# A written-out order of one long kernel: small products of TensorE gathered, first loads reordered

## The chip, the core and the metric

The kernel runs on one core of a Trainium2 chip. Its work is done by TensorE (PE; its weight loads are PEld), VectorE (DVE), ScalarE (ACT) and GpSimd (POOL); SyncE (SP) issues the DMAs. The metric is the device time of one execution in microseconds, the median of three runs. Times inside an execution are counted from the start of its span, the time from its first to its last instruction.

## What is computed

Three layers in a row, for batch B = 2, sequence S = 768, H = 8 heads of D = 64 (model width 512):

```python
# attention: each query sees 31 neighbours and 24 block summaries
k_sum = k.reshape(B, H, 24, 32, D).max(axis=3)
v_sum = v.reshape(B, H, 24, 32, D).mean(axis=3)
scores_l = where(|i - j| < 16, scale * q @ k.T, -1e9)
scores_s = scale * q @ k_sum.T + log(32)
a = softmax(concat(scores_l, scores_s))
x = a @ concat(v, v_sum)            # (B, S, 512)
# first feed-forward block, a convolution over the sequence as gate
h = relu(x @ w_in)                  # 512 -> 1024
gate = sigmoid(conv3(h, conv_w))
x = (h * gate) @ w_out              # 1024 -> 512
# second feed-forward block, with a layer norm
xn = (x - mean) / sqrt(var + 1e-6) * g_ln
out = x + relu(xn @ w_ch1) @ w_ch2  # 512 -> 2048 -> 512
```

Weights arrive as 64-bit floats and are turned into 32-bit ones on the chip.

## The kernel before

**How it is written.** A class `Plan` holds 2016 operations. Each has a name, the engines that may do it, a function that issues its few instructions, and the operations that it comes after. Buffers that are shared in turn are rings, such as `tr` (five PSUM banks), `x2` (two) and `ch` (two). The string `ORDER` at the head of the file lists every operation once, by its number, with the engine that does it: `13S` is operation 13 on SP, `44P` is 44 on TensorE, and V, A, G are DVE, ACT, POOL. `arrange` reads the string, and `trace` issues the operations in that order under manual scheduling. So each engine gets its instructions in exactly the order in which they stand in the string, and each executes its own in that order; waits come from data and buffers.

**Attention** goes by pairs j = 0 to 11, each 128 queries; two units u = 2j, 2j+1 of four heads belong to a pair. The names in the text:

- `kt`, `qt` (L373, early ones): transposes of k and q, made as products with an identity with 64 columns of the array. `kmb` (L394): maxima of k over blocks, on DVE. All six `kmb` of the first batch come ahead of the first scores.
- `M` (L479): writes the mask into a score bank; `S` (L487): scores of a pair, 64x64 products, accumulated on the mask; `X` (L541): row maximum; `E` (L553): exponent; `N` (L572): division by the sum; `P` (L582): transposes the probabilities, full size.
- `T` (L503): product with v for a pair, with 64 columns of the array. `H` and `L` (L269, L527) split its result in two 32-bit parts for the first feed-forward block.
- M0, M1, M10 to M13, M22 and M23 stand at the ends of the sequence and are two products of 64 columns each; the other M are one full-size product.

**The first feed-forward block** has 48 steps i. `h` (L719): x times w_in, in three parts a, b, c of four matmuls each; then on ACT and DVE relu, the three taps of the convolution (`b`, `c`), tanh, the gate `g` and its two parts `u`, `v`; and `x` (L796): six full-size products with w_out into two banks, for two halves. `h` and `x` of different steps stand between attention's products, from 45 us on.

**The second block.** `bn`, `ba`, `va`, `rs`, `nb` (L1034 to L1048) make mean and scale of a row; the power -0.5 is on POOL (L1046). `xn` (L1167 on ACT, L1170 on DVE) normalises, `tp` (L1205) transposes it on TensorE. Seven products `pr` (L1264) a step stand in for eight by a Strassen scheme; their results are added up on DVE (`pb` to `ph`, L1275). `ac` (L1343) multiplies by w_ch2 into accumulators. There are 16 steps, eight for each half of the batch, in an alternating order. `wa`, `wb` names are the weights' conversion (L639, L643, L648), `wo`, `wn`, `wl`, `wm` the low parts of the weights (L1075).

**The loads.** SP issues all loads in the order of the string: `lq`, `lk`, `lv` for q, k, v, `lw0` to `lw7` for w_in and `lw8` to `lw15` for w_out, each of 512 KB, `lc0` and `lc1` for the convolution's weights and the norm's.

The lines that make the string count:

```python
for word in order.split():
    o = self.ops[int(word[:-1])]
    o.eng = word[-1]
    assert o.eng in [e[0] for e in o.engs] and all(a in seen for a in o.after), o.name
    seen.add(o)
    self.done.append(o)
```

Of the kernel before, what the change touches and what calls it, by code (L numbers as in the profile page):

```python
# [8 lines left out]
104V 222V 40V 216V 199A 105A 233P 191P 204P 217V 106V 192A 51A 234P 235P 182V 101A 1P 102G 236V 243V 176A 205A 111A
159V 223V 86V 115S 237A 87A 55P 218P 177P 224V 110V 209V 88V 107A 225P 244A 108G 179V 200P 226V 238V 245V 246V 112V  # L10
228G 206P 219A 121S 201A 113A 180V 239V 247G 227P 207A 240V 114G 403P 402P 229A 202V 404P 89A 117A 230V 248P 241P 56V
412V 127S 231G 253P 413A 254P 405V 255P 424G 90G 266P 256A 232S 396S 359S 401S 242V 249V 267P 123A 406A 268P 116V 414V
122V 118V 257V 415V 279P 258V 128V 416G 280P 269A 281P 292P 282A 259V 293P 427P 417P 124V 407V 260A 426P 270A 428P
261V 283A 271V 284V 272V 294P 436V 262A 119A 120G 125A 273A 418A 305P 306P 437A 307P 126G 133S 263V 318P 139S 367S
408V 429V 274V 319P 308A 409V 295A 320P 264P 309V 430A 331P 397P 399P 296V 297V 285V 310V 438V 286A 275A 398A 431V
439V 135A 663S 425S 287V 276V 432V 311V 321A 312A 440V 265P 332P 410P 277P 333P 441P 344P 345P 134V 433V 298V 136V
322A 323V 313V 411A 129A 400A 299A 334A 288A 130V 300V 335V 324V 250P 278P 141A 131A 137A 346P 251V 140V 420G 252V
442V 289G 434P 419P 132G 290P 347A 421A 142V 138G 145S 291P 363P 368P 348A 325A 435A 301A 422V 360P 666P 423G 376S
151S 443P 667A 364A 336V 361V 302V 337V 349V 326V 350V 362V 365V 143A 444A 314A 446P 447P 369A 338A 351A 147A 315G
144G 370V 303P 448P 449A 450A 304P 352V 146V 339V 316P 459P 460P 371P 664P 372A 461P 462A 451V 445V 148V 152V 153A  # L20
327A 463G 377P 472P 328G 714S 380P 473P 149A 378A 474P 485P 317P 373V 452V 464V 383S 475A 381A 665V 465V 668G 150G
466A 340A 486P 672P 487P 329P 715P 498P 379V 382V 658V 499P 500P 453A 476A 659A 341V 154V 454V 385S 155A 501A 467V
477V 478V 502G 384V 671P 330P 156G 511P 342P 343P 488A 353A 479A 489A 694P 512P 695P 513P 386V 394V 375G 480V 387S
719S 354G 355P 357P 366G 389S 356A 503V 504V 490V 514A 673P 455A 524P 681V 505A 468A 515A 525P 456G 526P 696P 506V
374V 358V 388V 491V 457P 527A 682A 697V 528G 469G 458P 537P 481A 492A 470P 538P 698A 493V 660G 482G 539P 471P 516V
683V 684V 517V 529V 699V 674V 483P 494A 540A 395A 484P 552P 495G 496P 497P 553P 390V 530V 685G 507A 675A 518A 508G
519V 554P 555A 531A 541A 509P 510P 686P 676V 556A 520A 677V 391G 716A 565P 566P 567P 722P 721P 661V 704V 532V 705A
568A 723P 700V 678V 557V 521V 701G 689G 392V 542V 543V 393S 692S 731V 1129V 533A 544A 687A 569A 702P 679P 545V 578P
558V 724V 559A 534V 579P 580P 522P 523P 581A 732A 725A 535P 582G 560V 570V 583V 584V 706V 680V 707V 708G 591P 536P
592P 744P 720S 669S 693S 733V 670S 571V 546A 547V 726V 593P 745P 746P 703A 594A 572A 573V 747V 709P 710A 604P 605P  # L30
606P 548P 734V 735V 595A 596V 754V 736P 748A 727V 607A 585A 586V 749V 608V 550P 551V 609V 750V 617P 755A 618P 717P
619P 688P 711P 549A 620A 621A 561A 630P 562G 597V 718V 737A 598A 574A 756V 728V 729P 599V 610V 631P 871P 632P 690A
730A 633A 622V 623V 575V 691V 757V 611A 612V 751V 738P 563P 712V 713V 758V 662A 564P 872P 643P 873P 644P 587A 893G
# [1404 lines left out]
```

## Time and profile before

| | |
|---|---|
| runs (three) | 484.31, 484.78, 485.12 us; median 484.78 |
| the profiled execution | 484.99 us, its span 483.0 us |
| granted clock of TensorE, mean | 0.989 |
| busy: TensorE, DVE, ACT, POOL | 465.5, 364.6, 256.8, 124.4 us |

Busy time is the time in which an instruction of the engine runs. Matmuls follow each other in a pipeline, so one's length (391 ns for a 128x512 one) is longer than the distance to the next; what a matmul costs is read from the distance between starts. A matmul of 32-bit numbers can stand in the trace as two or more.

### The profile page before, as it was taken

To read this page: it belongs to the slowest core of one execution; us is meant where nothing else is said; L and a number is where in the kernel's file an instruction comes from. 1 tells how busy PE (TensorE), PEld (TensorE's weight loads), DVE (VectorE), ACT (ScalarE), POOL (GpSimd) and SP (SyncE) were. 2 spreads that over 40 slices of the span, in tenths; PEclk is the share of its full clock that TensorE was granted. 3 is DMA by queue.
4 is the path that set the end of the run, shared out by engine and by line. 5 is a ranking of instruction groups with operands and counts; after the bars stand their busy time and mean duration, and the time that the engine had idled before them with its cause. 6 is when DMAs were issued, how large, how long until landed. Compare 5 with 4: busy or idle time off the path is not lost.

```text
span 483.0 us, 8906 instructions
## 1 busy us (share of the span) xinstructions
PE 465.5 (96%) x3297; PEld 409.4 (85%) x3297; DVE 364.6 (75%) x776; ACT 256.8 (53%) x733; POOL 124.4 (26%) x154
## 2 busy tenths in 40 slices
PE   3999999999999999996999999999999999999997
PEld 3848888888889889885889998999899998889985
DVE  2799999998886778898798766778565768664553
ACT  4699987688676695767862425324332324322110
POOL 4545333631220331302531421102520202011000
PEclk9899999999999999997999999999999999999999
DMA  8996966404400211002201213202031120220213
GB/s 254 318 281 186 246 157 167 108 4 89 97 3 1 88 45 45 0 2 87 88 23 67 88 44 131 87 1 88 17 131 58 56 88 0 90 87 1 87 45 130
DMA packets 56043, 43.28 MB, mean 90 GB/s; under 512 B 34324, under 2 KB 46896, under 8 KB 56000
## 3 DMA queue, kind: packets, MB, share of 16 engines
q1 hardware_dynamic: 55856, 42.58, 30.8%
q8 instruction: 26, 0.43, 0.4%
q14 instruction: 17, 0.14, 0.1%
q10 hardware_dynamic: 144, 0.13, 0.1%
HBM read 39.22 MB, written 3.15 MB: 88 GB/s over the span
## 4 chain that ended last, share of the span: by engine, by line
PE 91%; DVE 3%; ACT 3%; DMA 2%; issue 1%; SPq 0%; POOL 0%; POOLq 0%; ACTq 0%
PE acc L1343 27%; PE ch L1264 23%; PE x L796 14%; PE h L719 13%; PE tr L503 2%; PE tr L582 2%; PE tr L719 2%; PE tr L487 2%; DMA early<-in_k_dram 2%; PE tr L366 1%; PE acc L1205 1%; PE tr L479 1%; PE x L841 1%; ACT xn L1167 1%; PE tr L373 1%
## 5 line engine op out<-in xcount | busy, mean ns | idle before, releaser
L1343 PE MATMUL acc<-w,cb 128*128 128x512 f32 x570 | 140.1, 391 | 0.0
L1343 PEld LDWEIGHTS acc<-w,cb 128*128 128x128 f32 x570 | 106.2, 188 | 18.8
L1264 PE MATMUL ch<-xb,w 128*128 128x384 f32 x384 | 78.1, 341 | 2.8 <-ACT xb L1239 1.4
L1264 PEld LDWEIGHTS ch<-xb,w 128*128 128x128 f32 x384 | 68.9, 190 | 6.4 <-ACT xb L1239 1.6
L719 PE MATMUL h<-xT,wi 128*128 128x256 f32 (+1 forms) x504 | 72.3, 287 | 0.0
L719 PEld LDWEIGHTS h<-xT,wi 128*128 128x128 f32 x504 | 66.7, 189 | 4.3 <-issue 0.7
L796 PE MATMUL x<-wo,ghi 128*128 128x512 f32 x192 | 61.7, 402 | 0.0
L1264 PE MATMUL ch<-xt,w 128*128 128x384 f32 x288 | 58.7, 341 | 0.0
L1275 DVE TENSOR_TENSOR u<-ch,u 128x384 f32<-128x384 f32 x64 | 35.2, 554 | 24.7 <-PE ch L1264 24.5
L1264 PEld LDWEIGHTS ch<-xt,w 128*128 128x128 f32 x288 | 51.9, 191 | 1.8
L752 DVE SCALAR_TENSOR_TENSOR c<-h,ccol,c 128x256 f32<-128x256 f32 x96 | 46.9, 500 | 3.7 <-POOL c L271 1.7
L1284 ACT ACTIVATE cb<-p 128x384 fp32r<-128x384 f32 x32 | 16.4, 519 | 45.8 <-DVE p L1275 34.4
L643 ACT ACTIVATE raw<-raw 128x512 f32<-128x512 f32 x32 | 21.4, 677 | 36.1 <-DMA raw<-in_moe_w_ch_dram 36.1
L796 PE MATMUL x<-wo,glo 128*128 128x512 f32 x96 | 38.0, 395 | 0.0
L796 PEld LDWEIGHTS x<-wo,ghi 128*128 128x128 f32 x192 | 32.2, 188 | 4.7 <-issue 0.4
L1284 ACT ACTIVATE cb<-u 128x384 fp32r<-128x384 f32 x32 | 16.3, 520 | 33.3 <-DVE u L1275 33.3
L553 ACT ACTIVATE prob<-tr,nm 128x120 f32<-128x120 f32 x96 | 33.2, 366 | 0.9 <-DVE nm L541 0.8
L731 ACT ACTIVATE h<-h 128x256 f32<-128x256 f32 (+1 forms) x42 | 16.2, 386 | 23.8 <-PE h L719 21.5
L1075 POOL TENSOR_TENSOR w<-raw,w 128x512 fp32r<-128x512 f32 (+1 forms) x12 | 15.0, 1254 | 51.2 <-ACT w L1142 45.0
L765 DVE SCALAR_TENSOR_TENSOR g<-c,h 128x256 f32<-128x256 f32 x48 | 22.5, 473 | 5.2 <-ACT c L757 5.0
L648 DVE SCALAR_TENSOR_TENSOR raw<-raw 128x512 uint32<-128x512 uint32 x32 | 23.1, 723 | 3.1 <-ACT raw L643 3.0
L783 POOL TENSOR_TENSOR glo<-g,ghi 128x256 fp32r<-128x256 f32 x19 | 15.5, 815 | 29.3 <-ACT ghi L776 21.4
(178 smaller groups left out, 772.2 us busy)
## 6 DMA issues: line engine op xcount, KB each, us to landing
raw<-in_moe_w_ch_dram SPq DMA_DIRECT2D x32, 512.0 KB, 3.4
wst<-in_moe_w_out_dram SPq DMA_DIRECT2D x8, 512.0 KB, 4.4
vw<-in_v_dram SPq DMA_DIRECT2D x20, 192.0 KB, 4.5
wst<-in_moe_w_in_dram SPq DMA_DIRECT2D x5, 512.0 KB, 7.7
s_q<-in_q_dram SPq DMA_DIRECT2D x8, 256.0 KB
early<-in_k_dram SPq DMA_DIRECT2D x3, 512.0 KB, 9.3
x2a<-in_moe_w_in_dram SPq DMA_DIRECT2D x3, 512.0 KB
early<-in_v_dram SPq DMA_DIRECT2D x3, 512.0 KB, 7.6
```

The costliest lines, as they stand in the source:

```text
L553: A.activation(out=pr[:, p, :], in_=sc[:, p * NK:(p + 1) * NK], func=AF.Exp, bias=nm[:, p:p + 1], scale=1.0, accum_out=sm[:, p:p + 1])
L643: A.activation(out=f, in_=f, func=AF.Prelu, scale=F64_SCALE, alpha=F64_SIGN)
L648: V.scalar_tensor_tensor(out=most, in0=most, scalar=3, in1=least, op0=ALU.logical_shift_left, op1=ALU.bitwise_or)
L719: T.matmul(live["h", i][:, 0:NM_], w_[:, c, f * 128:(f + 1) * 128], x_[:, c, 1:1 + NM_], start=(k_ == 0 and c == 0), stop=(k_ == 2 and c = ...
L731: A.activation(out=ht[:, lead:lead + NH], in_=live.pop(("h", i))[:, 0:NH], func=AF.Relu)
L752: V.scalar_tensor_tensor(out=ct, in0=ht[:, kk:kk + CH], scalar=ccol[:, kk * NF + f:kk * NF + f + 1], in1=ct, op0=ALU.mult, op1=ALU.add)
L765: V.scalar_tensor_tensor(out=gt, in0=ct, scalar=1.0, in1=ht, op0=ALU.add, op1=ALU.mult)
L796: T.matmul(x2ps[g, t], l[:, ts_], r[:, f, :], start=(f == 0 and j == 0), stop=(f == NF - 1 and j == 2))
L1264: T.matmul(bk[k], l[:, c, :], x_[:, c, :], start=j == 0 and c == 0, stop=j == 2 and c == 1)
L1275: lambda e: V.tensor_tensor(out=temp(to), in0=bk[k], in1=temp(x), op=ALU.add), after,
L1284: A.activation(out=half(0, r, y), in_=temp(src), func=AF.Relu)
L1343: T.matmul(acc[key], ct_[n][l][:, r, 128 * t:128 * t + 128], w2[s][k][:, r], start=first and j == 0, stop=done and j == 5)
```

## The change

Only the string `ORDER` differs: the same 2016 operations in another order, and some of them on another engine. The counts by letter go from 765 V, 476 A, 128 G, 85 S and 562 P to 751 V, 467 A, 150 G, 86 S and 562 P. Nothing else in the file is touched. Both lists keep every operation behind those that it comes after.

```diff
-13S 4G 5G 2G 8S 67S 61S 11S 10S 12S 14S 73S 91S 44P 79S 15S 7V 6V 68V 52V 69A 53A 70V 45A 46P 71A 63A 62V 64V 65A 47A
+13S 178G 2G 3G 157G 5G 67S 11S 10S 61S 12S 8S 14S 73S 44P 46P 79S 91S 15S 85S 45A 69A 68V 70V 25P 28P 71A 29A 47V 4G
...
```

SP's first loads were q0, conv, w1, w0, k1, k0, k2, q1, w2; they are now q0, w1, k1, k0, w0, k2, conv, q1, w2 (`w1` for `lw1`, and so on).

**DVE at the beginning**, from the first operation on a weight to the row maximum X0 (`nm`). `wst` is a staged piece of w_in, `ksum` the six maxima of k, `craw` the conv weights, `qb` and `kw` the scores' operands. Before:

```order
L639 TENSOR_SCALAR wst<-wst 128x512
L648 SCALAR_TENSOR_TENSOR wst<-wst 128x512
L648 SCALAR_TENSOR_TENSOR craw<-craw 24x128
L862 COPY crow<-craw 24x128
L394 TENSOR_REDUCE ksum<-tr 128x2x8
L394 TENSOR_REDUCE ksum<-x_182 128x2x8
L394 TENSOR_REDUCE ksum<-tr 128x2x8
L394 TENSOR_REDUCE ksum<-x_215 128x2x8
L394 TENSOR_REDUCE ksum<-x_224 128x2x8
L394 TENSOR_REDUCE ksum<-tr 128x2x8
L639 TENSOR_SCALAR wst<-wst 128x512
L648 SCALAR_TENSOR_TENSOR wst<-wst 128x512
```

After:

```order
L639 TENSOR_SCALAR wst<-wst 128x512
L394 TENSOR_REDUCE ksum<-x_181 128x2x8
L648 SCALAR_TENSOR_TENSOR wst<-wst 128x512
L394 TENSOR_REDUCE ksum<-tr 128x2x8 x2
L287 MEMSET warm 128x64
L394 TENSOR_REDUCE ksum<-x_209 128x2x8
L639 TENSOR_SCALAR craw<-craw 24x128
L394 TENSOR_REDUCE ksum<-x_227 128x2x8
L394 TENSOR_REDUCE ksum<-tr 128x2x8
L269 COPY kw_92<-kw_93 128x4x16
L269 COPY kw_93<-kw_92 128x4x16
L271 TENSOR_SCALAR qb_96<-tr 128x512
```

In both pieces the first row is the second weight piece, w0. Its second step now stands between the first maximum and the others, and the conv weights' last steps have gone further down.

**TensorE at the end of attention**, the two products T10 and T11 (L503; 16 products in the program's count, 32 in the trace's). Before:

```order
L719 MATMUL h<-xT,wi_87 128x258 x8
L503 MATMUL tr<-probT,vw_98 64x64 x16
L719 MATMUL h<-xT,wi_88 128x258 x4
L796 MATMUL x_2016<-wo_617,ghi 128x512
L796 MATMUL x_2016<-wo_618,ghi 128x512
L796 MATMUL x_2016<-wo_617,glo 128x512
L503 MATMUL tr<-probT,vw_99 64x64 x16
L796 MATMUL x_2515<-wo_617,ghi 128x512
```

After:

```order
L719 MATMUL h<-xT,wi_87 128x258 x8
L719 MATMUL h<-xT,wi_88 128x258 x4
L503 MATMUL tr<-probT,vw_98 64x64 x16
L503 MATMUL tr<-probT,vw_99 64x64 x16
L796 MATMUL x_2536<-wo_670,ghi 128x512
```

The two blocks of 64-column products have become one, with one border ahead and one behind.

**DVE in the change from the first to the second feed-forward block**, from the statistics of the last two row tiles (`st`, `mv`) to the normalised rows `xn` of the second half of the batch; `w` is the low part of a weight, `ts`, `sg` and `xb` belong to the first half's operands. Before:

```order
L1034 BN_STATS st<-x2b 128x6 x2
L1037 BN_AGGR mv<-st 128x2
L1075 TENSOR_TENSOR w_3300<-raw,w_3299 128x512
L1037 BN_AGGR mv<-st 128x2
L1043 TENSOR_SCALAR rs<-mv 128x6
L1075 TENSOR_TENSOR w_3300<-raw,w_3299 128x512
L1224 TENSOR_TENSOR ts<-sg,acc 128x256
L1075 TENSOR_TENSOR xb_2540<-acc,xb_2539 128x4x128
L1224 TENSOR_TENSOR ts<-sg,ts 128x256
L1048 SCALAR_TENSOR_TENSOR rs<-mv,rs 128x6
L1224 TENSOR_TENSOR ts<-acc,ts 128x256
L1170 TENSOR_SCALAR xn<-x2b,mv,rs 128x512
```

After:

```order
L1034 BN_STATS st<-x2b 128x6 x2
L1037 BN_AGGR mv<-st 128x2 x2
L1043 TENSOR_SCALAR rs<-mv 128x6
L1075 TENSOR_TENSOR w_3300<-raw,w_3299 128x512
L1224 TENSOR_TENSOR ts<-sg,acc 128x256
L1075 TENSOR_TENSOR xb_2529<-acc,xb_2528 128x4x128
L1224 TENSOR_TENSOR ts<-sg,ts 128x256
L1048 SCALAR_TENSOR_TENSOR rs<-mv,rs 128x6
L1075 TENSOR_TENSOR w_3300<-raw,w_3299 128x512
L1224 TENSOR_TENSOR ts<-acc,ts 128x256
L1170 TENSOR_SCALAR xn<-x2b,mv,rs 128x512
```

The low part of the weight (`w_3300`) that stood between the two aggregates now stands behind the variance's last step (L1043). The `xn` in the last row is the first half of its pair before, and the second half after; the other half is ACT's. On TensorE, the two groups of transposes of this pair (`tp101`, `tp100`) have a product pr001 and pr002 between them before, and follow each other after; `tp111` has moved from behind pr004 to behind pr010.

## Rows read from the trace of the kernel before

**Rows 1.** The page, part 1: busy us, share of the span, instructions.

```profile
PE 465.5 (96%) x3297; PEld 409.4 (85%) x3297; DVE 364.6 (75%) x776; ACT 256.8 (53%) x733; POOL 124.4 (26%) x154
```

**Rows 2.** Stretches: length, busy us (instructions) of PE, PEld, DVE, ACT, POOL, PEclk, DMA.

```profile
0.00:45.00 45.00, 35.44 (x488) 25.66 (x489) 32.11 (x75) 32.90 (x103) 22.81 (x46) 0.96 0.92 261
45.00:218.10 173.10, 173.10 (x1525) 152.42 (x1525) 152.38 (x351) 129.92 (x451) 50.29 (x65) 1.00 0.32 78
218.10:222.90 4.80, 2.39 (x15) 1.74 (x13) 4.59 (x13) 2.79 (x6) 2.87 (x2) 1.00 0.31 95
222.90:229.80 6.90, 5.54 (x21) 5.12 (x20) 5.16 (x11) 5.48 (x10) 0.00 (x0) 0.51 0.27 86
229.80:239.30 9.50, 8.92 (x54) 8.25 (x53) 7.82 (x17) 7.73 (x15) 5.10 (x6) 1.00 0.36 111
239.30:473.80 234.50, 234.50 (x1179) 211.87 (x1178) 159.58 (x309) 77.97 (x150) 43.30 (x38) 1.00 0.19 62
```

**Rows 3.** Waits of TensorE: us in total, times, longest us.

```profile
PE tr L373 <- DMA early<-in_q_dram: 5.1, 1, 5.1
...
PE ch L1264 <- ACT xb L1239: 1.4, 1, 1.4
PE acc L1205 <- ACT xn L1167: 1.4, 1, 1.4
PE ch L1264 <- DVE xb L1075: 1.0, 1, 1.0
```

**Rows 4.** Timeline of TensorE, 119.5 to 161.6 us: start, us, instructions.

```profile
120.72 2.08 PE L503 MATMUL tr<-probT,vw 120*64 120x64 f32 x64
122.74 0.74 PE L719 MATMUL h<-xT,wi 128*128 128x256 f32 x4
...
158.60 0.40 PE L796 MATMUL x<-wo,glo 128*128 128x512 f32 x1
158.93 1.15 PE L503 MATMUL tr<-probT,vw 120*64 120x64 f32 x32
160.01 0.74 PE L796 MATMUL x<-wo,ghi 128*128 128x512 f32 x2
160.59 0.39 PE L796 MATMUL x<-wo,glo 128*128 128x512 f32 x1
160.82 0.63 PE L796 MATMUL x<-wo,ghi 128*128 128x512 f32 x2
161.28 0.40 PE L796 MATMUL x<-wo,glo 128*128 128x512 f32 x1
```

**Rows 5.** Timeline, 0 to 30 us, with idle time before and its releaser.

```profile
6.37 0.43 DVE L639 TENSOR_SCALAR wst<-wst 128x512 uint32<-128x512 uint32 x1 [5.28 <-DMA wst<-in_moe_w_in_dram]
...
9.29 0.85 DVE L639 TENSOR_SCALAR wst<-wst 128x512 uint32<-128x512 uint32 x1 [1.50 <-DMA wst<-in_moe_w_in_dram]
...
11.09 1.77 PE L373 MATMUL x<-ident,early 128*64 128x128 f32 x16 [2.64 <-DMA early<-in_k_dram]
...
17.24 1.29 DVE L394 TENSOR_REDUCE ksum<-x 128x16 f32<-128x512 f32 x2 [0.29 <-ACT kw L267]
...
21.47 0.64 DVE L541 TENSOR_REDUCE nm<-tr 128x4 f32<-128x480 f32 x1
```

**Rows 6.** Timeline of DVE, 42 to 45 us.

```profile
43.22 1.28 DVE L527 TENSOR_TENSOR xT<-tr,xT 128x512 fp32r<-128x512 f32 x2
```

**Rows 7.** Timeline of the change of blocks, 219 to 225 us.

```profile
219.66 0.66 DVE L1075 TENSOR_TENSOR w<-raw,w 128x512 fp32r<-128x512 f32 x1
...
222.86 0.54 DVE L1170 TENSOR_SCALAR xn<-x2b,mv,rs 128x512 f32<-128x512 f32 x1
...
223.72 0.81 ACT L1167 ACTIVATE xn<-x2b,rs 128x512 f32<-128x512 f32 x1
```

**Rows 8.** The page, part 5: busy us, mean ns of one, idle before.

```profile
L1275 DVE TENSOR_TENSOR u<-ch,u 128x384 f32<-128x384 f32 x64 | 35.2, 554 | 24.7 <-PE ch L1264 24.5
...
L648 DVE SCALAR_TENSOR_TENSOR raw<-raw 128x512 uint32<-128x512 uint32 x32 | 23.1, 723 | 3.1 <-ACT raw L643 3.0
```

More of the change, by code (lines that the diff above doesn't have):

```diff
@@ L9 @@
[L9 to L33, printed above, removed]
@@ new lines @@
+1202V 1078V 1055V 1142V 1088P 1146V 1020A 1032P 1148V 1044V 1089A 1033P 1090G 1066V 1056A 1067A 1079V 1068V 1057V
+1091V 1099P 1045P 1046P 1100P 1080A 1092V 1101P 1058P 1102A 1069A 1070G 1103A 1093A 1059P 1112P 1209V 1147V 1081V
+1113P 1104V 1082A 1083V 1094V 1143V 1200V 1114P 1205A 1071P 1115A 1105V 1206G 1072P 1116A 1117V 1084P 1095A 1106A
+1149V 1096V 1085P 1107V 1118V 1097P 1108A 1119A 1201V 1109V 1098P 1120V 1207A 1121A 1110P 1210V 1122V 1111P 1208V
+1123P 1278V 1125P 1124A 1150V 1126A 1211P 1212P 1279A 1152V 1213A 1151V 1153V 1154V 1218A 1280V 1155G 1273A 1214V
@@ new lines @@
+1286S 1219V 1215V 1315P 1217G 1156V 1274V 1224A 1216V 1281S 1220A 1225V 1222A 1221G 1227P 1226P 1223V 1288A 1287V
+1317P 1289V 1228A 1316A 1229V 1283A 1290G 1233A 1239A 1296A 1282V 1319P 1232V 1318V 1284V 1323P 1320V 1285V 1325P
+1321A 1235A 1295A 1324V 1291G 1334P 1322V 1293G 1292G 1297A 1294G 1301G 1326V 1327V 1241P 1330P 1299V 1335V 1300V
+1230V 1338P 1331V 1303S 1309S 1240A 1248A 1328A 1242P 1342P 1332A 1339A 1336A 1298A 1333V 1231V 1337V 1234V 1329V
+1340P 1236G 1237A 1254A 1302G 1238G 1363P 1361P 1362P 1243A 1305A 1304V 1341V 1343V 1306V 1310V 1244V 1245V 1246V
@@ new lines @@
+1249V 1247G 1346P 1348P 1347V 1255A 1257P 1250A 1251G 1311A 1252A 1344A 1353P 1256P 1350V 1349V 1307A 1258A 1351A
+1253G 1345V 1312V 1366P 1357P 1263A 1259V 1260V 1354V 1262V 1308G 1261V 1264V 1365P 1364P 1355A 1313A 1267A 1358V
+1268V 1356V 1431S 1367P 1359A 1360V 1314V 1436S 1433A 1265A 1368V 1432V 1369P 1370V 1266G 1371P 1392P 1372V 1373A
+1375P 1377P 1352V 1374V 1376V 1379V 1437V 1378V 1390P 1382P 1434V 1391V 1393V 1383V 1398P 1386P 1400P 1402P 1384A
+1385V 1387V 1438A 1380A 1435A 1445A 1388A 1439V 1403A 1404P 1440V 1441V 1389V 1446A 1405V 1443V 1447A 1449V 1451V
@@ new lines @@
+1410P 1412P 1396P 1401V 1444V 1381V 1450G 1442G 1411V 1413V 1482S 1487S 1394P 1395V 1414V 1484A 1489A 1448A 1421P
+1429P 1422V 1399V 1397V 1406P 1483V 1407V 1488V 1485V 1408A 1490V 1409V 1415A 1491A 1428P 1453P 1454A 1426P 1430P
+1452V 1486V 1423A 1424V 1417P 1418V 1419A 1497A 1496A 1420V 1455P 1456V 1425P 1492V 1494G 1495G 1461P 1501V 1493V
+1462V 1457P 1458V 1500V 1463P 1427P 1504S 1510S 1499A 1416V 1465V 1464V 1459A 1460V 1468P 1466A 1506A 1467V 1469V
+1472P 1473V 1505V 1507V 1470A 1508A 1503G 1474A 1475V 1509V 1479P 1476P 1498A 1512A 1528P 1529V 1471V 1511V 1480P
@@ new lines @@
+1513V 1502G 1522S 1514A 1523V 1515V 1516S 1477P 1530P 1481P 1478P 1532P 1524A 1531V 1533V 1536P 1538P 1551P 1552P
+1518A 1517V 1525V 1519V 1526A 1534A 1527G 1537V 1535V 1539V 1520A 1621S 1540V 1521V 1541A 1553P 1554P 1547P 1548V
+1549A 1542V 1543P 1626S 1544V 1545A 1623A 1628A 1557P 1559P 1555P 1546V 1550V 1558V 1560V 1565P 1567P 1566V 1627V
+1568V 1622V 1556P 1572P 1629V 1569V 1573V 1624V 1580P 1625G 1630A 1631G 1576P 1561P 1586P 1632V 1633G 1636A 1635A
+1637A 1582P 1577V 1562V 1640V 1590P 1592P 1588P 1639G 1594P 1672S 1563A 1641G 1634G 1564V 1578A 1638A 1579V 1673V
@@ L100 @@
+1987P 1985A 1986V 1988V 1989A 1996P 1991P 1999P 2000P 1990V 1992V 1993A 1994V 2002P 1997P 2006P 2012P 2010P 2014P
+2001V 2015V 2003V 2004P 2005V 1998P 2007V 2011V 2013V 2008P 2009V
 """
```

138 lines of the change are left out of this document (68 added, 70 removed).

## The prediction

> **What bounds the kernel now.** I read the page first, then the busy time by stretches, the waits of TensorE, and the timeline at three places. TensorE is busy 465.5 of 483.0 us [rows 1], so the question is what stands in the other 17.5 us, and whether all of the busy time is work. The stretches divide it [rows 2]. In the first 45 us TensorE is busy 35.44 us and idle 9.6. From 45 to 218.1 it is busy for all 173.10 us, and from 239.3 to 473.8 for all 234.50: there nothing waits, and a new order can win only by making the same instructions pack better. Between the two lies the change from the first feed-forward block to the second (218.1 to 239.3, 21.2 us), with 4.35 us idle and, in its middle, 6.9 us at a granted clock of 0.51, the lower level of 1.2 GHz; TensorE had been busy for only half of the 4.8 us before it. The waits name the holes [rows 3, 5]: 5.1 us for the first q, 2.64 for the first k, and in the change of blocks 1.4, 1.4 and 1.0 us for ACT and DVE.
>
> **Part 1, borders of small products: 1.35 us.** Attention's products use 64 columns of the array, everything else (128x512 and the like) all of it. The timeline prices a border by distances between starts [rows 4]. A glo product followed by another full-size one takes 0.23 us to the next start (160.59 to 160.82); before the 64-column product at 158.93 the same takes 0.33 (158.60 to 158.93). So entering costs 0.10. The two ghi after it take 0.58 (160.01 to 160.59) instead of 0.46 (160.82 to 161.28): leaving costs 0.12, rounded down to 0.11 for the other places. A product with v takes 1.08 alone (158.93 to 160.01), but two in a row take 2.02 (120.72 to 122.74), not 2.16: another 0.14.
>
> I counted blocks of neighbouring 64-column products on TensorE in the two lists: 27 before, 21 after. The first eight are the same size; the difference is six joins after them: M11 with M10, M12 with M13, S6 with S7, T3 with T4, T10 with T11, and S9 behind T6 and T7 (M22/M23 are parted, and M23 joins S10: no change). Six joins by 0.21 are 1.27, and the two pairs of T give 2 x 0.14 more: 1.55 us. All of it lies on the path, since TensorE never waits in this stretch.
>
> Two joins put different shapes side by side (T7 before S9, S10 before M23), which the trace of before never shows. The nearest rows are T beside T, where no border is paid, and T beside a full-size product, where 0.21 is paid. That leaves 1.13 to 1.55. I take 0.1 each, half way: 1.35 us. The Trainium skill, TensorEngine Tiling (Array Packing), Tiling Modes, says that changing the tiling mode, not just the tile, drains TensorE; by that 64x64 beside 128x64 is a change too and pays, and the sum would be 1.13, where the two rows alone would allow 1.55.
>
> **Part 2, the first loads: 0.7 us.** Before, the queue is q, conv weights, two pieces of w_in, k1, k0, k2. DVE starts on the first piece at 6.37 and on the second at 9.29, and k1 lets TensorE go on at 11.09 [rows 5]. So a 512 KB piece comes about every 1.8 to 2.9 us. After, k1 and k0 stand before the second w_in piece: k1 in the third place by about 9.3, k0 by 11.1, w_in by 12.7, and k2 as before. TensorE's transposes start 1.8 us sooner. But this doesn't all reach the end, because DVE's list holds the second w_in piece (w0) ahead of all six reductions of k. From 12.7 DVE must do: 0.43 for w0, six reductions at 0.65 (two took 1.29) [rows 5], 0.69 for w0's second step, 0.6 for four small ones, two of 512 columns at 0.65 each, 0.42 and 0.69 for the next weight: 8.0 us. The first row maximum X0 then starts at 20.7, not 21.47: 0.8 us. From X0 to the pair L1, L2, which frees the first product h0a (21.47 to 43.22) [rows 5, 6], DVE runs nearly without a break. Its list holds 51 operations there before and 49 after: nine leave (4.6 us by the means of their kinds) and seven come (4.4). So h0a starts 1.0 to 1.2 sooner. But one transposition (P6, 0.44 us) now comes behind h0a and not ahead: 0.7 net. ACT holds 3 us less work ahead of L2 than before, and is no bound. Bounds: 2.0 if w0 lands 1.2 sooner, and -0.5 if it lands at 14 us.
>
> The conv weights wait behind k2, and what they feed is first used by b0, after h0a; that is covered by some 20 us. Of the moves between engines 22 go to POOL (128 operations to 150). POOL is busy 50 of 173 us in the long stretch [rows 2], and TensorE reads none of these at once; they cost nothing while that cover is there, about 1 us each on the path where it is not.
>
> **Part 3, the change of blocks: 1.3 us.** Before, DVE does one correction of w2 (0.66 us at 219.66) before the last step of the variance; POOL's power waits for that, then DVE normalises the first half of a pair (222.86, 0.54) and ACT the second (223.72, 0.81) [rows 7]. TensorE waits 1.4 us for it [rows 3]. After, that correction stands behind the variance: everything below comes 0.66 sooner. ACT now does the first half and DVE the second: the scale that let DVE begin at 222.86 is there by 222.2, and 0.81 + 0.54 behind it, with some 0.15 between, end at about 223.7, where the pair ended at 223.72 + 0.81 = 224.53: 0.85 sooner. If only this wait shrinks, 0.85 is won; if the later waits from 229.8 to 239.3 go too (9.50 - 8.92 = 0.58 us) [rows 2], 1.4. I take 1.3, since the second group of transposes (tp100) now fills what was waiting time for the next operand, and the group that waited later (tp111) stands behind two products that are ready. Its lower bound is -0.3: POOL now makes the sums of the next w1 (four of about 0.85 us in a row, then two corrections of 1.4), and the product pr011 needs the first of these corrections.
>
> **The sum.** 1.35 + 0.7 + 1.3 = 3.35 us. The profiled execution took 484.99 us (span 483.0 and 2.0 around it), so 481.6; the median of the runs lies 0.2 below it: **481.4 us**.
>
> **Rivals.** (a) Only the borders. If X0 is held by the next weight (its piece is the ninth in the queue in both lists) and pr001 by its own operand xt, 2 and 3 give nothing: 484.78 - 1.35 = 483.4. For it: DVE's next weight step stands right before X0 in the new list. Against: no row of before shows an engine waiting for that piece.
>
> (b) Slower: DVE in the long last stage. Two PSUM banks serve the products pr, so a product waits until DVE has added up the last but one. In the old list a product follows with just one other product between (1.05 us of cover) 12 times from pr020 on; in the new list 19 times, and runs of four products without an accumulation between stand there 6 times, before never. An addition takes 554 ns, and one weight step of 723 ns [rows 8] ahead of it already makes 1.28 us: a wait of 0.23. It decides from 3.35 / 19 = 0.18 us at each such place; at 0.35 us it costs 6.7 and the kernel takes 484.8 - 3.35 + 6.7 = 488. Against it: DVE is busy only 159.58 of 234.50 us there, and in before none of the 12 places made TensorE idle [rows 2].
>
> (c) No change: smaller waits of this sort, and of POOL's in 3, eat all that is won: 484.8.
>
> (d) The slow stretch disappears. TensorE was busy 5.54 us in it [rows 2]; at the upper level, 2.4 GHz, these would take half, so up to 2.8 us go, half of it into waits for the same operands: 480 or less. Against it: the waits before the stretch shrink only from 3.8 to some 3 us.
>
> **How the numbers follow.** Less than 0.2% (1 us) can't be told from no change here. The three terms 0.56 (480.0 to 482.8), (a) 0.18 (483.4, still faster by 0.3%), (d) 0.04, (c) 0.11 (483.8 to 485.7), (b) 0.11 (486 to 490). So faster 0.78, same 0.11, slower 0.11. The range: upward through (a) into the near half of (c), 484.4; downward by the bounds of 1 (1.55), 2 (2.0) and 3 (1.4), 4.95 in all, and a part of (d), 479.0.
>
> **What would show it.** Right: T10 and T11 as one row of 64 matmuls with 2.0 us to the next start; TensorE busy nearly without a break from 45 to the change of blocks, and that change reached 2 us sooner; X0 near 20.7; the transposes that wait for xn released about 5.6 us after the last product of the first block (before 6.4), and the first accumulation some 20 us after it (before 21.1). Wrong: idle time of TensorE ended by DVE at products pr after 240 (b), a DVE gap before X0 ended by a weight's DMA (a), or a stretch at 0.5 of another length in the change of blocks (d).

## The result, and the profile after

The changed kernel takes 489.17 us (median of six runs, 487.88 to 491.29) against 483.93 (six runs): 1.0109 times as long, 95% interval 1.008 to 1.0139. It was forecast at 481.4 and is slower by 1.1%. The profiled execution took 489.72 us, its span 487.9.

The page, part 1, of the changed kernel:

```profile
PE 466.0 (96%) x3297; PEld 407.6 (84%) x3297; DVE 375.4 (77%) x760; ACT 253.8 (52%) x725; POOL 142.3 (29%) x177
```

Beside [rows 1], TensorE has as much to do as before. POOL has 18 us more, as 22 more operations on it should give. DVE is the odd one: 16 instructions fewer, and yet 10.8 us more busy time.

Stretches of the changed kernel (columns as in [rows 2]), cut at the end of the first feed-forward block:

```profile
45.00:215.90 170.90, 170.90 (x1526) 152.07 (x1525) 153.24 (x344) 128.01 (x446) 58.30 (x80) 1.00 0.31 78
215.90:236.90 21.00, 17.30 (x86) 15.35 (x85) 19.40 (x37) 14.87 (x28) 12.69 (x12) 0.84 0.31 100
236.90:260.00 23.10, 19.14 (x97) 16.36 (x96) 21.60 (x33) 10.88 (x20) 10.20 (x7) 1.00 0.15 46
260.00:300.00 40.00, 39.58 (x198) 35.23 (x197) 32.19 (x61) 15.61 (x31) 7.58 (x6) 1.00 0.18 56
300.00:473.00 173.00, 171.96 (x858) 154.81 (x857) 111.80 (x205) 53.09 (x103) 31.09 (x28) 1.00 0.19 64
```

The first block still has no hole, and ends 2.2 us sooner (215.9 instead of 218.1). The first accumulation ac002 starts at 236.87, before at 239.27: 2.4 us ahead. From there to the end of the span it takes 251.0 us, before 243.7. Then, where TensorE before was busy without a break [rows 2], it is idle for 4.0 of 23.1 us, and for 1.5 us more behind that, while DVE is busy for 21.60 of the 23.1. The waits of TensorE (us in total, times, longest):

```profile
PE tr L373 <- DMA early<-in_q_dram: 5.4, 1, 5.4
PE acc L1343 <- DVE xb L1075: 2.1, 1, 2.1
PE ch L1264 <- DVE u L1275: 2.1, 3, 1.0
PE x L841 <- DMA early<-in_v_dram: 1.9, 1, 1.9
PE ch L1264 <- ACT xb L1239: 1.3, 1, 1.3
```

The second, the third and the fourth are new beside [rows 3]. Two end with DVE, one with v's first load. What DVE and POOL did around the longest of DVE's (timeline of the changed kernel; rows of DVE and POOL in order of time, and the row of TensorE behind the wait):

```profile
237.80 2.19 POOL L1075 TENSOR_TENSOR xt<-ts,xt 128x768 fp32r<-128x768 f32 x1
238.19 2.07 DVE L639 TENSOR_SCALAR raw<-raw 128x512 uint32<-128x512 uint32 x1
240.19 0.55 DVE L1275 TENSOR_TENSOR u<-ch,p 128x384 f32<-128x384 f32 x1
...
241.24 0.68 DVE L648 SCALAR_TENSOR_TENSOR raw<-raw 128x512 uint32<-128x512 uint32 x1
241.84 0.42 DVE L639 TENSOR_SCALAR raw<-raw 128x512 uint32<-128x512 uint32 x1
...
245.67 1.85 POOL L1075 TENSOR_TENSOR xt<-ts,xt 128x768 fp32r<-128x768 f32 x1
246.04 1.89 DVE L1287 SCALAR_TENSOR_TENSOR cb<-p,cb 128x384 fp32r<-128x384 f32 x1 [0.34 <-ACT cb L1284]
247.46 1.64 POOL L1075 TENSOR_TENSOR w<-raw,w 128x512 fp32r<-128x512 f32 x1
247.85 1.79 DVE L648 SCALAR_TENSOR_TENSOR raw<-raw 128x512 uint32<-128x512 uint32 x1
...
251.49 0.68 DVE L1075 TENSOR_TENSOR xb<-acc,xb 128x512 fp32r<-128x512 f32 x1
...
252.32 1.62 PE L1343 MATMUL acc<-w,cb 128*128 128x512 f32 x6 [2.12 <-DVE xb L1075]
```

Instructions of one line and one shape take DVE 0.42 us at 241.84 and 2.07 at 238.19, and those of another line 0.68 at 241.24 and 1.79 at 247.85. The long ones began while POOL was in an instruction with two operands in SBUF, and ended after it. The row at 240.19, which has an operand in PSUM (`ch`), has its usual length. Each long one pushes DVE's list back; the last but one row is yp12, which the accumulation ac003 waits for.

To count this, each DVE instruction was compared with the lower quartile of its own shape in the same run; what is above is called stretched. In the trace before, 28 instructions are longer by over 0.2 us, 15.5 us in all; after, 50 and 31.4 us. Every one of these 78 overlaps an instruction of POOL. The place where it counts lies between the first addition of the first step, pb00, and that of the third, pb02: there DVE is idle for 1.3 us in the changed kernel (4.8 before). The last column of the table holds every excess over the quartile, also those under 0.2 us. The first rows of this table are the two kernels; the others are the runs below. (Successive instructions overlap a little, so the columns may add up to more than the distance.)

| us, pb00 to pb02 | distance | DVE's own work | stretched |
|---|---|---|---|
| before | 28.6 | 25.7 | 0.9 |
| changed | 30.9 | 24.6 | 8.1 |
| e3 new order, old engines | 31.7 | 25.2 | 4.9 |
| e4 old order, new engines | 29.4 | 24.0 | 6.3 |
| e10 before, POOL subtracting | 32.9 | 25.7 | 6.0 |
| e13 changed, POOL quiet | 25.3 | 24.6 | 0.3 |
| e17 changed, five given to DVE | 30.0 | 27.8 | 2.2 |

The new list gives DVE 1.1 us less to do there, and DVE needs 2.4 us longer for it.

### The profile page after: what moved, and what is told of

Read it like the earlier page. It is cut to its first block, busy times and chain, and to the rows that moved or that the text cites. A ratio compares the mean times of both kernels' runs of the same rounds, so it can differ in the third digit from the quotient of the medians.

```text
span 487.9 us, 8924 instructions
## 1 busy us (share of the span) xinstructions
PE 466.0 (96%) x3297; PEld 407.6 (84%) x3297; DVE 375.4 (77%) x760; ACT 253.8 (52%) x725; POOL 142.3 (29%) x177
## 3 DMA queue, kind: packets, MB, share of 16 engines
q1 hardware_dynamic: 55916, 42.68, 30.9%
## 4 chain that ended last, share of the span: by engine, by line
PE 80%; DVE 6%; DMA 3%; ACT 3%; SPq 2%; issue 2%; POOL 2%; POOLq 0%; DVEq 0%
PE acc L1343 22%; PE ch L1264 19%; PE x L796 14%; PE h L719 12%; PE tr L582 2%; PE tr L503 2%; PE tr L487 2%; PE tr L719 2%; DMA early<-in_v_dram 2%; PE x L841 1%; SPq L677 1%; PE tr L366 1%; DVE cb L1287 1%; DMA raw<-in_moe_w_ch_dram 1%; PE tr L479 1%
## 5 line engine op out<-in xcount | busy, mean ns | idle before, releaser
L719 PE MATMUL h<-xT,wi 128*128 128x256 f32 (+1 forms) x504 | 70.2, 284 | 0.0
L752 DVE SCALAR_TENSOR_TENSOR c<-h,ccol,c 128x256 f32<-128x256 f32 x96 | 49.1, 523 | 3.4 <-POOL c L271 1.8
L1275 DVE TENSOR_TENSOR u<-ch,u 128x384 f32<-128x384 f32 x64 | 35.3, 552 | 20.7 <-PE ch L1264 20.1
L1075 POOL TENSOR_TENSOR w<-raw,w 128x512 fp32r<-128x512 f32 (+1 forms) x12 | 14.6, 1215 | 72.7 <-ACT w L1142 38.4
L783 POOL TENSOR_TENSOR glo<-g,ghi 128x256 fp32r<-128x256 f32 x26 | 20.3, 783 | 49.2 <-ACT ghi L776 38.8
L1287 DVE SCALAR_TENSOR_TENSOR cb<-p,cb 128x384 fp32r<-128x384 f32 x32 | 22.1, 693 | 7.8 <-ACT cb L1284 7.6
L1287 DVE SCALAR_TENSOR_TENSOR cb<-u,cb 128x384 fp32r<-128x384 f32 x32 | 20.9, 660 | 8.1 <-ACT cb L1284 8.1
```

Source lines behind the costliest of these rows:

```text
L719: T.matmul(live["h", i][:, 0:NM_], w_[:, c, f * 128:(f + 1) * 128], x_[:, c, 1:1 + NM_], start=(k_ == 0 and c == 0), stop=(k_ == 2 and c = ...
L752: V.scalar_tensor_tensor(out=ct, in0=ht[:, kk:kk + CH], scalar=ccol[:, kk * NF + f:kk * NF + f + 1], in1=ct, op0=ALU.mult, op1=ALU.add)
L783: on[e].tensor_tensor(out=glo, in0=live.pop(("g", i)), in1=live["ghi", i].bitcast(F32), op=ALU.subtract)
L1275: lambda e: V.tensor_tensor(out=temp(to), in0=bk[k], in1=temp(x), op=ALU.add), after,
L1287: V.scalar_tensor_tensor(out=half(1, r, y), in0=temp(src), scalar=0.0, in1=half(0, r, y).bitcast(F32), op0=ALU.max, op1=ALU.subtract)
```

## The experiments

Theory 1: POOL's instructions with two operands in SBUF stretch DVE's, and DVE sets the pace from 226 to 257 us. Theory 2: the new order itself is bad (DVE's additions behind runs of four products, or yp12 too late). Theory 3: POOL is slow at the operations moved to it, and its results come late. The times of before that belong to the runs are 484.14 (e1 to e4), 483.68 (e5 to e8), 483.96 (e9 to e12), 484.12 (e13 to e16) and 482.93 us (e17); brackets hold 95% intervals of the ratio to before.

**Which part of the list: e1 and e2.** The lists were joined behind the 1213th operation, at the last transposes of the first half of the batch.

```diff
# e1, against the changed list: from operation 1214 on, the old list
-... 1211P 1212P 1279A 1152V 1213A 1151V 1153V 1154V 1218A 1280V 1155G 1273A ...
+... 1211P 1212P 1279A 1152V 1273A 1151V 1280V 1218A 1213A 1153V 1286S 1154V ...
# e2, against the old list: the reverse
```

> New list up to the last transposes ahead of the second block's first product (opening, attention, first feed-forward block), old list and old engines from there on. By the traces the new list was 2.4 us ahead at the start of ac002 and lost 4.7 us from 240 to 260 us and 2 more later. If all of the loss is made by the second part of the list, this takes about 481.6 us (484.0 less 2.4; 481 to 482.5). If the first part sows it (buffers, loads or weights that are late), it takes 486 or more.

> The mirror: old list up to the same point, new list and new engines behind it. If the second part makes the loss alone, about 491 us (489.2 plus the 2.2 us that the first part had won; 490 to 492). If the first part sows it, 485 or less.

Measured: e1 481.19 us, 0.9942 [0.9919, 0.9965]; e2 491.44, 1.0152 [1.0121, 1.0183]. The first part of the new list gives 2.95 us, the second takes 7.3 (e2 against before) to 8.0 (the changed kernel against e1), and neither needs the other for it. e1 is faster than both kernels.

**Order or engines: e3 and e4.** Behind the same point, 28 operations are POOL's in the new list alone, and 19 in the old one alone. e3 keeps the new order and gives each operation its old engine; e4 keeps the old order and gives each its new one.

```diff
# e3, against the changed list
-1286S 1219V 1215V 1315P 1217G 1156V 1274V 1224A ...
+1286S 1219V 1215V 1315P 1217V 1156V 1274V 1224V ...
# e4, against e1: the reverse
```

> New list throughout, but in its second part (from the last transposes ahead of the second block) each operation on the engine that it had before: 28 operations leave POOL, 19 come back to it. Theory 1 (DVE's instructions are stretched while POOL works on two SBUF operands): most of the 4.7 us between 240 and 260 come back and DVE's stretched time there falls from 8.6 us to about 1: 484 to 486 us. Theory 2 (the order itself: DVE's additions behind runs of four products, and yp12 at the end of DVE's list): little comes back, 488 to 490 us. Theory 3 (POOL's own chain of sums of the next weight is too long): 486 to 488.

> As the first of these four (new first part, old order in the second), but each operation of the second part on the engine that the new list gives it (62 operations of the list change their engine or its place beside POOL). Theory 1 (stretching by POOL): slower than the first of the four by 3 us or more, 485 to 488 us, with stretched DVE instructions at 232 to 260 us. Theory 2 (order): within 1 us of it, 481 to 483 us.

Measured: e3 489.85 us, 1.0119 [1.0096, 1.0141]; e4 487.56, 1.008 [1.0055, 1.0104]. e4, 6.4 us slower than e1 by the engines alone, speaks for theory 1. e3 went against its expectation, and looked like theory 2; but the stretched time had not fallen to 1 us either. It was 4.9 between pb00 and pb02, mostly because `yt10` and `yt11` are POOL's in both lists and the new order lays DVE's L639 (2.08 us) and L1287 (1.89 us) beside them.

**Is it yp12's place: e5.**

```diff
# against the changed list: 1263 is xp12, 1264 yp12, 1307 hd10, 1345 op01
-... 1307A 1258A 1351A 1253G 1345V 1312V 1366P 1357P 1263A ... 1261V 1264V ...
+... 1307A 1263A 1258A 1351A 1253G 1345V 1264V 1312V 1366P 1357P ... 1261V ...
```

> New list with two operations moved: on ACT xp12 to right behind hd10, on DVE yp12 to right behind op01, eight DVE operations sooner (about 248 instead of 251.5 us). In the new list TensorE waited 2.1 us at ac003 for yp12. If yp12's place is the cause (theory 2a), that wait goes and the time falls by about 2 us, to 487. If DVE as a whole is behind from 237 to 257 us (theory 2b), the wait only moves on to pr020 to pr022, which need DVE's next results, and the time stays within 0.7 us of 489.2.

Measured 488.67 us, 1.0106 [1.0084, 1.0129]: 0.5 less than the changed kernel. By the distance between starts, less what the products themselves take, TensorE lost 1.7 instead of 2.3 us ahead of ac003, but 1.6 instead of 1.0 ahead of pr022: the wait moved on. DVE as a whole was behind.

**The same length on POOL, one operand: e6, e7 and e9.**

```diff
# in short: a helper at the three places of the second block where POOL subtracts or adds;
# e6 in the changed list, e7 in e4's, e9 in e3's
-on[e].tensor_tensor(out=out, in0=x, in1=y, op=op)
+if e == "G":
+    G.tensor_copy(out, x)
+    G.tensor_copy(out, y)
+else:
+    on[e].tensor_tensor(out=out, in0=x, in1=y, op=op)
```

These three kernels leave out the subtractions and additions that POOL did in the second block.

> New list, but in the second block each subtraction or addition with two operands in SBUF that POOL does is replaced by two copies of one operand each, of about the same length together (1.4 us for 128x512); the low parts made on POOL and the sums made there then hold wrong numbers. DVE's work and POOL's time stay as they are. If stretching by POOL's two-operand instructions makes the loss (theory 1), DVE's stretched time at 220 to 260 us falls from 8.6 us to below 1.5 and 3 us or more come back: 486 or less. If the order alone makes it (theory 2), 488.5 or more though the stretching is gone. If the stretching stays, copies collide as well, and the run says nothing between 1 and 2.

> The same replacement in the list of the fourth run (new first part, then old order on the new engines; 487.6 us, 6.4 more than with the old engines). There no order was changed, only engines. Theory 1 (stretching): back to within 1.5 us of the old engines, 481 to 483 us. Theory 3 (POOL is slower than DVE at the same operation, and what waits for its result comes later): 486 or more, since POOL's time is the same.

> The third run (new order, old engines in its second part; 489.9 us) with the replacement of POOL's two-operand instructions by two copies each, as in the sixth and seventh; the low parts and sums made on POOL hold wrong numbers. In the third run DVE was stretched by 4.9 us between its additions pb00 and pb02 although the old engines were back. If stretching makes this loss too (theory 1), 485 us or less. If the new order is slow by itself (theory 2), 488 or more.

Measured: e6 483.32 us, 0.9994 [0.9978, 1.0011], 5.9 less than the changed kernel; e7 483.64, 0.9999 [0.998, 1.0017], 3.9 less than e4; e9 487.27, 1.0084 [1.0062, 1.0107], 2.6 less than e3. All three fall, but copies still stretched DVE (3.6 us from pb00 to pb02 in e6), and the first of two copies doesn't wait for ACT, so that a part could be theory 3's. e9 left theory 2 open.

**The change of blocks alone: e8.** The join of e1, 65 operations later: behind pr006, the sixth product of the first step in that list, and ahead of the first accumulation. POOL's sums of the next w1 in the new order (sa1 to sd1, wn10) are in this part.

> New list up to the change of blocks and through it as far as pr004 (1278 operations, with the moved correction of w2, both groups of transposes and the exchanged normalisation), then the old list. It measures the third term of the forecast by itself, beside 481.2 us for the new list up to the start of the change of blocks. If that term is right, 1.3 us less: about 480. If the change of blocks is worth nothing or a loss, 481.2 or more; if the loss of the new list is sown there, 484 or more.

Measured 484.47 us, 1.0023 [1.0002, 1.0043]: 3.3 more than e1. The transposes of the last pair did come sooner (tp100 6.8 us behind tp020, in e1 11.2), but DVE was stretched by 4.8 us from 220 to 240 (before 0.5), TensorE then waited 2.2 us for one addition, and its granted clock was at 0.50 for the 3.4 us behind that wait. So this run can't price the change of blocks without the collisions.

**The collision by itself: e10 and e11.** In the old list, POOL is idle from 251.4 to 260.7 us. There it gets work on a free tile that nothing reads.

```diff
# against the old kernel, behind POOL's wo11 (in short: e10 has the first loop, e11 the second)
+scr = p2.tile([128, 2, DM], F32, tag="xn", name="xn", bufs=1)[:, 0, :]
+G.memset(scr, 0.0)
+for _ in range(6):                                                  # e10
+    G.tensor_tensor(out=scr, in0=scr, in1=scr, op=ALU.subtract)
+for _ in range(15):                                                 # e11
+    G.memset(scr, 0.0)
```

> The kernel before, with work added to POOL alone where POOL stood idle for 9.3 us (251.4 to 260.7 us): a MEMSET of a free 128x512 tile and six subtractions of that tile from itself, two operands in SBUF, about 1.4 us each; nothing reads the tile. Theory 1: DVE's instructions with operands in SBUF are stretched there by some 0.7 us each time, 4 us in all; DVE has about 1.5 us to spare, so TensorE loses 2 us or more and the time is 486 or more. Theories 2 and 3: nothing waits for this work, and the time is that of before, 483 to 484.5.

> The control to the run before it: in the same place a MEMSET and fifteen more MEMSETs of the same tile, about 0.5 us each, which read nothing and fill about the same time on POOL. Theory 1 (two operands read from SBUF collide): no DVE instruction stretched, the time of before, 483 to 484.5 us. If any work of POOL's slows DVE, it is as slow as the run before it.

Measured: e10 491.1 us, 1.015 [1.012, 1.0179]; e11 483.68, 1.0001 [0.9985, 1.0018]. Timeline of e10, rows of POOL and DVE, and the row of TensorE behind the wait:

```profile
251.28 8.34 POOL L1080 TENSOR_TENSOR xn<-xn 128x512 f32<-128x512 f32 x6
...
252.07 1.39 DVE L1292 SCALAR_TENSOR_TENSOR cb<-p,cb 128x384 fp32r<-128x384 f32 x1
253.38 1.52 DVE L1075 TENSOR_TENSOR w<-raw,w 128x512 fp32r<-128x512 f32 x1
254.83 2.70 DVE L1292 SCALAR_TENSOR_TENSOR cb<-u,cb 128x384 fp32r<-128x384 f32 x2
257.46 1.26 DVE L639 TENSOR_SCALAR raw<-raw 128x512 uint32<-128x512 uint32 x1
258.64 1.52 DVE L1075 TENSOR_TENSOR xb<-sg,xb 128x512 fp32r<-128x512 f32 x1
...
260.68 1.65 PE L1269 MATMUL ch<-xb,w 128*128 128x384 f32 x4 [3.88 <-DVE u L1280]
```

and of e11, the same instructions of DVE:

```profile
250.50 9.15 POOL L1080 MEMSET xn<- 128x512 f32 x15
...
251.32 0.55 DVE L1292 SCALAR_TENSOR_TENSOR cb<-p,cb 128x384 fp32r<-128x384 f32 x1
251.78 0.68 DVE L1075 TENSOR_TENSOR w<-raw,w 128x512 fp32r<-128x512 f32 x1
252.39 1.02 DVE L1292 SCALAR_TENSOR_TENSOR cb<-u,cb 128x384 fp32r<-128x384 f32 x2
253.71 0.52 DVE L639 TENSOR_SCALAR raw<-raw 128x512 uint32<-128x512 uint32 x1 [0.31 <-DMA raw<-in_moe_w_ch_dram]
254.15 0.68 DVE L1075 TENSOR_TENSOR xb<-sg,xb 128x512 fp32r<-128x512 f32 x1
```

Six subtractions of POOL, and six instructions of DVE in step with them, each longer by 0.84 us (1.39 instead of 0.55, 1.52 instead of 0.68, 1.26 instead of 0.42): 5.0 us. TensorE then waits 3.88 us. The stretches of e10 show what the wait costs on top (columns as before):

```profile
251.28:259.57 8.29, 5.52 (x27) 4.39 (x25) 8.29 (x8) 3.02 (x6) 7.90 (x6) 1.00 0.40 127
259.57:266.39 6.82, 5.71 (x16) 5.12 (x17) 5.87 (x12) 0.52 (x1) 1.12 (x3) 0.50 0.00 0
```

Behind it, TensorE's granted clock is at 0.50, the lower level of 1.2 GHz, for 6.8 us; 5.71 busy us at that level are 2.9 lost, and with the wait that makes 6.7 of the 7.1 us by which the time grew. Nothing waits for POOL's added work, so theory 3 has no part in it; the MEMSETs, as long on POOL, cost nothing.

**v's load: e12.**

```diff
# against e1: 15 is v's first load, 14 the second q, 73 the third piece of w_in
-... 12S 8S 14S 73S 44P 46P 79S 91S 15S 85S ...
+... 12S 8S 14S 15S 73S 44P 46P 79S 91S 85S ...
```

> The first run (new list up to the second block, then the old one; 481.2 us) with v's first load three places sooner in SP's queue, ahead of the third, fourth and sixth piece of w_in. In the new list TensorE waited 1.5 to 1.9 us for it at vb0. If TensorE's chain sets the time of h0a, 1 to 2 us less: about 480. If DVE's chain sets it (X0 to L2, without a gap), the wait goes and the time stays within 0.5 us of 481.2; if the pieces of w_in are now late for DVE, 482 or more.

Measured 481.91 us, 0.9971 [0.9953, 0.9988]: nothing won beside e1. The product with v no longer waits, but the next one on TensorE, P0, then waits 2.3 us for DVE's `prob`.

**POOL quiet: e13 to e16.** The same four combinations of order and engines as the changed kernel, e1, e3 and e4, with what copies had left in doubt taken away. Of each two-operand operation of POOL's only 16 columns are done (4 of each row where the operand has rows); the rest is left out, and MEMSETs fill its time.

```diff
# in short: the same helper at the same three places
+n = 4 if len(out.shape) > 2 else 16
+G.tensor_tensor(out=out[..., 0:n], in0=x[..., 0:n], in1=y[..., 0:n], op=op)
+G.memset(out.bitcast(F32), 0.0)
+G.memset(out.bitcast(F32), 0.0)
```

> New list. In the second block each two-operand instruction of POOL's is cut to 16 of its columns and followed by two MEMSETs of its whole output, about the same length together (1.4 us for 128x512), with the same waits; low parts and sums made on POOL hold wrong numbers. The copies of the sixth run still stretched DVE by 3.6 us from 220 to 260 and did not wait for ACT; this leaves neither. If stretching is all of the loss, the time is that of the old second part treated alike (next run) within 1 us, about 481. If the new order loses by itself, 483.5 or more: the rest is the order's.

> The first run (new first part, old order and old engines behind; 481.2 us) with POOL made quiet in the same way: the base of the other three. DVE was stretched there by only 0.9 us between pb00 and pb02, so 480.5 to 481.5 us is expected by every theory.

> The third run (new order on the old engines; 489.9 us, and 487.3 with copies) with POOL made quiet. Stretching alone: within 1 us of the run before it, about 481 to 482. Order by itself: 485 or more, since nine more operations are on DVE there than in the new list, and the order was not made for that.

> The fourth run (old order on the new engines; 487.6 us, and 483.6 with copies) with POOL made quiet. Stretching alone: 480 to 482 us. If POOL's slowness at the moved operations counts as well, 483 or more.

| second part, us | as written | POOL quiet |
|---|---|---|
| old order, old engines (e1, e14) | 481.19 | 481.19, 0.9949 [0.9926, 0.9973] |
| new order, new engines (changed, e13) | 489.17 | 479.67, 0.991 [0.9884, 0.9937] |
| new order, old engines (e3, e15) | 489.85 | 484.72, 1.0014 [0.9995, 1.0034] |
| old order, new engines (e4, e16) | 487.56 | 483.05, 0.9969 [0.9951, 0.9987] |

The stretch of e13 that answers to the one above with 4 us of idle time:

```profile
236.90:260.00 23.10, 22.67 (x119) 20.39 (x118) 18.11 (x37) 10.85 (x22) 6.74 (x16) 1.00 0.14 45
```

TensorE is busy for 22.67 us instead of 19.14, and DVE does four instructions more in 3.5 us less. The old list, where little was stretched at this place, gets nothing from a quiet POOL (e14), so that the treatment by itself gives nothing; the changed kernel gets 9.5 us. Without the collisions the new list is not slow, but as fast as the old one or faster, and theory 2 falls for it, since order and runs of four products are all there. Not every expectation held. e15 and e16 came out 3.5 and 1.9 us above e14, near or in the range that was set for a cost of order or of POOL's slowness by itself (485 or more, 483 or more). So beside the collisions (5.1 us between e3 and e15, 4.5 between e4 and e16) half of the new list has a price of its own, which the whole of it hasn't; which operations make it is open.

**Five operations given back to DVE, with all the work in: e17.** 1301, 1238, 1253, 1308 and 1266 are wn10, yt10, yt11, wo10 and ys12.

```diff
-... 1294G 1301G 1326V ... 1302G 1238G 1363P ... 1253G 1345V ... 1308G ... 1266G
+... 1294G 1301V 1326V ... 1302G 1238V 1363P ... 1253V 1345V ... 1308V ... 1266V
```

> New list, nothing left out; five subtractions that POOL does between 232 and 256 us (wn10, yt10, yt11, wo10, ys12) are given to DVE, in the same places of the order. Doing them costs DVE 3 x 0.68 + 2 x 0.95 = 3.94 us by the lengths of the same shapes on DVE; the DVE instructions that began while these five ran on POOL were stretched by 1.08, 0.64 + 1.66, 1.34, 1.11 and 1.10 = 6.9 us. If the collisions are priced rightly, DVE is 3 us shorter and the time 485.5 to 487. If giving work back to DVE costs what the work takes, 489 to 493.

Measured 487.58 us, 1.0092 [1.0075, 1.0109], where 485.5 to 487 were expected. The median is 1.6 us below the changed kernel's, but that of before was 1.0 us lower as well in these runs (482.93 against 483.93), and the intervals of the two ratios overlap: a gain is not shown by the time. The traces show the parts. Between pb00 and pb02 the stretched time fell by 5.9 us (8.1 to 2.2, other subtractions of POOL being still there), DVE's own work rose by 3.2, and the distance fell from 30.9 to 30.0. Behind the start of ac002 the span is 3.3 us shorter than the changed kernel's. Ahead of it 2.3 us are lost: pr005 now waits 2.1 us for DVE, which it did not before, and the granted clock is at 0.50 for 3.4 us from 232.19 on. So DVE has fewer collisions and more work, and e1 stays the better kernel.

## Why the prediction was wrong

**The step that failed** is the sentence in Part 2 on the moves between engines: 22 operations go to POOL, "TensorE reads none of these at once; they cost nothing while that cover is there". It counted the moved work as time on POOL, judged the cover by the long stretch of the first block, and asked whether TensorE waits for it. What POOL's work does to DVE it did not ask; that term stood at nothing. The work is paid by DVE: a two-operand instruction of POOL holds up a DVE instruction that reads SBUF beside it, and from 226 to 257 us DVE is what the products wait for. The price is some 7 to 8.5 us, against a forecast of nothing. A quiet POOL gives back 9.5 us (489.17 less 479.67). Of the 9.9 us between the two profiled spans 5.8 lie behind the start of ac002 and 2.7 in the change of blocks, where some 1.2 go with a shorter slow stretch (Part 3; whether a quiet POOL shortens it is open); the other 1.4 lie in the opening, which that edit does not touch.

The moves are not all of it. In the second block 28 operations go to POOL and 19 leave it, and the new order on the old engines collides too (5.1 us between e3 and e15). What counts is which instructions of POOL and DVE stand beside each other, and the prediction priced that for neither the engines nor the order. Its argument against rival (b), that DVE is busy for only 159.58 of 234.50 us, failed in the same place: a mean over the last stage, where the loss was made between 237 and 257 us with DVE busy for 21.60 of 23.10.

The rows that the prediction was made from could have said so: in the trace before, 28 DVE instructions were stretched, though only 1 us of it lay where it counts. [rows 5] shows one of them: L639 takes 0.43 us at 6.37 and 0.85 at 9.29, there beside a subtraction of POOL's (L660, 8.57 to 9.86), and Part 2 reckoned with 0.43. A group's mean hides it. [rows 8] gives 554 ns for the additions L1275, which have an operand in PSUM and are never stretched; the lines that are, L1287, L639, L648 and L1075, were not compared one by one. The rule was to be had as well: the Trainium skill, SBUF — State Buffer, Who interferes with whom, says that a DVE instruction with two inputs in SBUF contends with a GpSimd instruction that reads SBUF, not with one that only writes, and that the second to come is blocked for the whole of the first. e10 and e11 agree, 0.84 us for each subtraction and none at the MEMSETs for the instructions with two inputs. It also says that copies and `tensor_scalar` can, when their operands meet certain conditions, run in a mode that takes both ports and then contends with GpSimd; e11's TENSOR_SCALAR at 253.71, 0.52 instead of 0.42 us beside the MEMSETs, agrees, though no run here shows which mode it ran in.

**Part 1, the borders, 1.35 us:** right, and too small. From the first h to the last x TensorE needed 172.6 us before (44.82 to 217.43) and 170.75 after (44.44 to 215.19), with P6, 0.44 us, now among it: 2.3 us. The pair T10, T11 stands as one row of 64 with 2.01 us to the next start, as forecast (timeline of the changed kernel):

```profile
155.74 2.08 PE L503 MATMUL tr<-probT,vw 120*64 120x64 f32 x64
157.75 0.73 PE L796 MATMUL x<-wo,ghi 128*128 128x512 f32 x2
```

2.3 us is beyond the upper bound of 1.55. One term was left out: two S in a row save time of their own, as two T do. S6 and S7 take 1.80 us together (86.20 to the next start at 88.00), one alone 0.98 (107.19 to 108.17): 0.16. Which joins hold the rest isn't settled.

**Part 2, the first loads, 0.7 us:** w0 reached DVE at 11.39 and not 12.7, and X0 started at 18.78, not 20.7. But h0a came only 0.4 us sooner in this execution. The step didn't look at v: in the new list TensorE comes to the product with v before its load. Timeline of the changed kernel:

```profile
18.81 1.05 PE L487 MATMUL tr<-kw,qb 64*64 64x120 f32 x32
21.79 3.58 PE L841 MATMUL x<-early,ind 128*24 128x512 f32 x4 [1.92 <-DMA early<-in_v_dram]
25.29 0.65 PE L582 MATMUL tr<-ident,prob 128*120 128x128 f32 x4
```

and of e1, which has the same opening:

```profile
21.47 1.90 PE L841 MATMUL x<-early,ind 128*24 128x512 f32 x4 [1.53 <-DMA early<-in_v_dram]
23.30 0.65 PE L582 MATMUL tr<-ident,prob 128*120 128x128 f32 x4
```

In the changed kernel's profile the clock falls to its lower level as this wait ends, for 3.4 us, and the product takes 3.58 us; in e1's it doesn't, and h0a starts at 42.12, 2.7 us sooner than before. The profile of before has such a fall too, 3.4 us from 11.34 on. Like with like: in the traces without a fall in the opening, h0a starts at 43.90 and 44.33 with the old opening (e11, e10) and between 42.12 and 43.21 with the new one (e1, e3 to e7, e9, e13 to e17), 0.7 to 2.2 us sooner. So 0.7 lies at the lower end; e12 shows that the wait for v itself is hidden behind DVE.

**Part 3, the change of blocks, 1.3 us:** the mechanism was right, and eaten. The transposes that wait for xn were released 5.9 us behind the first block (215.90 to 221.82; 5.6 forecast, 6.4 before). But from the start of the last x to ac002 it was 21.8 us before and 21.7 after. With POOL quiet it is 19.0 in the new list (e13) and 20.9 in the old one (e14), both with a slow stretch of 3.4 us: the new order is worth 1.9 us there. Not all of the 2.7 us between the changed kernel and e13 are collisions: e1 and e12 have one list behind the opening, and take 22.1 us with a slow stretch of 6.8 and 20.9 with one of 3.4.

**Rival (d):** in this profile the slow stretch stayed at 6.8 us. In other traces it is 3.4 us, with the old order (e12, e14) and with the new one (e3, e13), and 6.8 in others of both (e1, e5); that the new list shortens it is not shown.

**The sum** without the collisions is 479.67 us: 4.3 less than before, where 3.35 were forecast. The clock has a part in that: its mean is 0.996 to 0.999 in the four runs of e13 and 0.990 to 0.993 in those of the changed kernel. How much of this follows from the collisions and how much is chance isn't shown, so that the nearness of 4.3 to 3.35 says little of the three terms, of which each came out larger. **Rival (b)** had the sign, the place (TensorE idle behind 240, ended by DVE) and the size (488). It named DVE rightly as what the products wait for, but not what put DVE behind: its runs of four products are in e13, where TensorE is idle for only 0.7 us from ac002 on. It got 0.11.

## What to carry to other kernels

Before work is moved to POOL, look for DVE instructions of one shape that have two lengths, and at what POOL does meanwhile: the price of a two-operand instruction there can be paid by DVE, here 0.84 us a piece in e10 and up to 1.65 in the changed kernel (2.07 instead of 0.42, beside a subtraction of 128x768), more than the 0.68 us in which DVE does a 128x512 subtraction itself. It counts only where DVE sets the pace, so price such a move by DVE's gaps in that stretch and not by the mean share of either engine. A list of orders and engines is one thing: with POOL quiet, half of the better one on half of the other takes 484.72 and 483.05 us (e15, e16), where the whole ones take 479.67 and 481.19. The best kernel with all its work, e1, takes the new list up to the change of blocks, and the old one from there.
